# Gated loop attention with a multiplicative feed-forward: the looks wait for unit 0's last gated product, and unit 3's pieces begin after fifteen halves

## The chip, the cores and the metric

The kernel runs on one core of one Trainium2 chip. Its time is the device time of one execution in microseconds, and the median of several runs is compared. A profile of one more execution gives the start and length of every instruction on the engines: TensorE (PE, with its weight loads as PEld), VectorE (DVE), ScalarE (ACT), GpSimd (POOL) and SyncE (SP), which here only issues DMAs.

## What is computed

```python
def _attn_ref(q, k, v, a_re, a_im):          # (4, 8, 768, 48) each
    mag = np.sqrt(a_re * a_re + a_im * a_im)
    scale = np.minimum(mag, 0.999) / (mag + 1e-06)
    a_re_n, a_im_n = (a_re * scale, a_im * scale)
    for t in range(S):
        new_re = ar * S_re - ai * S_im
        new_im = ar * S_im + ai * S_re
        kv = np.einsum('bhd,bhe->bhde', k[:, :, t], v[:, :, t])
        S_re, S_im = (new_re + kv, new_im)
        y[:, :, t] = np.einsum('bhd,bhde->bhe', q[:, :, t], S_re)

def _moe_ref(x, w1, w2, w3, w_out):          # x: (3072, 384)
    a = x @ w1                               # 384 -> 1024
    b = x @ w2
    h = a * b @ w3                           # 1024 -> 1024
    return (h @ w_out).astype(np.float32)    # 1024 -> 384
```

A linear recurrence with a complex gate for each channel and step (the gate's magnitude is kept below 0.999) gives y. Its heads, put side by side, are the rows x of a feed-forward part in which two projections are multiplied element by element and then go through w3 and w_out.

## The kernel before

The 4 x 768 steps are cut into eight units of 384 steps, two for each batch entry, and each unit into three chunks of 128 steps. The weights come as 64-bit words and are rounded to 32 bits on the chip while the first 100 us run; w3 and w_out are multiplied into one matrix w3o.

Four kinds of work belong to each unit, and those of neighbouring units overlap:

- The gates (function gates): a chain of about thirty steps on ScalarE and VectorE over tiles of 128 x 1152. For unit u+1 it begins with two ScalarE passes over the real part (lines 594 and 596), then im times a factor (line 600, after the transfer of the imaginary part), its square (line 604), and a logarithm of that on ScalarE (line 609; a helper, line 586, records all these ScalarE steps). Later come scans (lines 628 and 687), products with k and q (654 and 656), and four products with cosine and sine (717, 719, 723 and 726). The transfer of the next unit's imaginary part is issued on SP's queue behind line 719, the moves of the finished tiles into the layout KL and QL behind that (line 736).
- The pieces: transposes of the scaled keys (line 766) with a ScalarE copy KT for each (768), the state products kv (830) with an addition on VectorE (836), the scores sc (780) with a masked copy (783), and the outputs y (813) with a ScalarE copy xT (815). Transposes, kv and y share two PSUM buffers (pool ps_v), so each of them waits until the copy of the last but one is out.
- The feed-forward: sixteen halves of three matmuls each (line 852). Halves of the first kind end in a ScalarE copy a (857), those of the second in the gated product ab on VectorE (859). Unit 0's output part is plain matmuls o (948). In the other units two tiles are done together with seven products p1, p2, p4, p6, p7, p5 and p3 in place of eight (912), for which VectorE forms four sums So (887).
- The looks (check_weights): GpSimd goes over all weights and the first two units' gates in 84 groups. It loads each with its own DMA queue (1042 and 1045), tests it in two to four operations (1066 to 1071) and adds up in the tile seen (1050); nothing else runs on GpSimd in that time. Near the end the function judge reads seen on VectorE (1170), sums over partitions on TensorE (1177) and sets a flag by which a general version is run if a test failed.

The order of TensorE's work is written out by hand. The function unit(u, rest, ahead) takes the pieces of unit u and the feed-forward items of unit u-1, puts the first `ahead` items in front, and spreads the pieces evenly among the others; the list AHEAD gives that number for each unit. A planner (run, with book, fits and fill) then goes through that sequence with a clock for each engine and the durations in TIMES, and puts the gate steps of the next unit on ScalarE and VectorE, and the DMAs on SP, where by its clocks they fit. Instructions on one engine run in the order so found. The looks are a generator called from the same loop, first when unit 2's part has begun; on GpSimd they stand in order behind each other, whatever the planner's clocks say.

The memset that opens the looks (line 1034) writes seen into memory that the weights' rounding used, and so waits for the last rounding on VectorE (line 1014). Waits beyond what the data ask for can be put in by hand:

```python
def behind(ins, key):
    if key in last:
        tc.add_manual_dep(ins.ins, last[key].ins.name, BEHIND, reason="room")
```

where the dictionary last holds instructions that were noted under a key.

Of the kernel before, what the change touches and what calls it, by code (L numbers as in the profile page):

```python
# [17 lines left out]
OP = mybir.AluOpType  # L18
# [358 lines left out]
def kernel(  # L377
# [36 lines left out]
    nc = tc.nc  # L414
# [8 lines left out]
    KF = FF // P  # L423
# [5 lines left out]
    TT = S // 2  # L429
    UC = TT // C  # L430
    NU = 2 * B
    AHEAD = [0, 3, 12, 12] + [8] * (NU - 4)
    LO, HI = 32, D - 32
    PASS, WIDE, SCAN, LAND, SLACK, LATE, RING, LOOK, NEAR, EARLY = 1.17, 1.4, 1.05, 1.8, 0.7, 1.2, 8, 4.0, 4, 2
    LOOKS = 3
# [59 lines left out]
    g_t, L_t, xT_t, ab_t, T_t, KT_t = {}, {}, {}, {}, {}, {}  # L495
# [34 lines left out]
    last = {}  # L530
# [4 lines that stand above are left out]
# [309 lines left out]
    def ffn_ab(u, j):  # L844
        got = []

        def half(w):
            if j == 0 and not got:
                ab_t[u] = one.tile([P, KF, TT], FP, tag="ab", name="ab")
            m = ps_m.tile([P, TT], FP, tag="mm", name="m")  # L850
            for f in range(KD):
                nc.tensor.matmul(out=m, lhsT=w[:, j * P // WB, f, j * P % WB:j * P % WB + P], rhs=xT_t[u][:, f],  # L852
                                 start=(f == 0), stop=(f == KD - 1))
            with tc.high_priority():
                if not got:
                    got.append(two.tile([P, TT], FP, tag="a", name="a"))
                    nc.scalar.copy(out=got[0], in_=m)  # L857
                else:
                    nc.vector.tensor_tensor(out=ab_t[u][:, j], in0=m, in1=got[0], op=OP.mult)  # L859
        return [("ab1", lambda: half(w1s)), ("ab2", lambda: half(w2s))]  # L860


# [157 lines left out]
    def words(src):  # L1020
        return (src if src.dtype == FP else src.bitcast(I32)).rearrange("(i p) m -> p i m", p=P)
# [3 lines left out]
    def check_weights(late):  # L1025

        groups = [("gate", u, f, x) for u in range(2) for f in range(KD) for x in range(2)]
        for w in (w1, w2, w3t, wo):
            if w.dtype != FP:
                src = words(w)  # L1030
                step = next(n for n in range(512, 0, -2) if src.shape[2] % n == 0)
                groups += [(w, src[:, i, j:j + step], step) for i in range(src.shape[1]) for j in range(0, src.shape[2], step)]
        seen = s_t["seen"] = late.tile([P, 256], BF, name="seen")
        nc.gpsimd.memset(seen, 0.0)  # L1034

        def load(group):
            got = late.tile([P, 512], FP, tag="look", name="look", bufs=LOOKS)
            if group[0] == "gate":
                _, u, f, x = group
                b, h = divmod(u, 2)  # L1040
                t0 = h * TT + x * (TT // 2)
                nc.gpsimd.dma_start(out=got[:, 0:TT // 2], in_=art[b, :, DG * f:DG * (f + 1), t0:t0 + TT // 2].rearrange(
                    "h d s -> d h s"))
            else:
                nc.gpsimd.dma_start(out=got.bitcast(I32)[:, 0:group[2]], in_=group[1])  # L1045
            return got

        def add(x):
            n = x.shape[1]
            nc.gpsimd.tensor_tensor(out=seen[:, 0:n], in0=seen[:, 0:n], in1=x, op=OP.add)  # L1050
            counted[0] += n

        tt, ts = nc.gpsimd.tensor_tensor, nc.gpsimd.tensor_scalar
        raws = [load(group) for group in groups[:LOOKS - 1]]
        for i, group in enumerate(groups):
            yield
            if i + LOOKS - 1 < len(groups):
                raws.append(load(groups[i + LOOKS - 1]))
            raw = raws.pop(0)
            if group[0] == "gate":  # L1060
                n = TT // 2
                x, y, low, high = raw[:, 0:n], raw[:, n:2 * n], SMALL, LARGE
            else:
                w, src, step = group
                x, y, low, high = raw[:, 1:step:2], raw[:, 0:step:2], MIN_SQ, MAX_SQ if w is w3t else None
                tt(out=x, in0=x, in1=x, op=OP.mult)  # L1066
            if high is not None:
                ts(out=y, in0=x, scalar1=high, scalar2=None, op0=OP.is_le)  # L1068
            ts(out=x, in0=x, scalar1=low, scalar2=None, op0=OP.is_ge)  # L1069
            if high is not None:  # L1070
                tt(out=x, in0=x, in1=y, op=OP.mult)  # L1071
            add(x)
# [14 lines left out]
    got = {}  # L1087
# [113 lines left out]
    def ffn(u, parts=1):  # L1201
        ab = [x for j in range(KF) for x in ffn_ab(u, j)]
        last = [(("o", "half")[parts - 1] if n == parts - 1 else "part", f) for n, f in enumerate(ffn_out(u, UC - 1, parts))]
        if u == 0:
            return ab + [(("part", "half")[n], f) for t in range(UC) for n, f in enumerate(ffn_out(u, t, parts))]


        def pair(*tiles):
            return [(f"p{p}", f) for p, f in zip((1, 2, 4, 6, 7, 5, 3), out_pair(tiles))]

        own, thirds = ((u, 0, False), (u, 1, False)), ((u - 1, UC - 1, True), (u, UC - 1, False))
        if u == 1:
            return ab + [("so", lambda: (out_sums(own), last[0][1]()))] + pair(*own)
        got = ab + [("sum", lambda: out_sums(own))] + pair(*own)
        if u % 2:
            return got + [("sum", lambda: out_sums(thirds))] + pair(*thirds)
        return got[:len(ab) + 6] + [("keep", lambda: keep(u))] + got[len(ab) + 6:]
# [8 lines left out]
    def unit(u, rest, ahead):  # L1226

        if u == 1:
            return [("begin", u)] + mixed([x for p in pieces(u) for x in p], rest, FILLS[1])
        seq = [("begin", u)] + rest[:ahead]  # L1230
        rest = rest[ahead:]
        p = pieces(u) + [[]]
        n = len(p)
        first = [i * (len(rest) - 2) // (n - 1) for i in range(n)] + [len(rest)]
        for i in range(n):
            seq += rest[first[i]:first[i + 1]] + p[i]
        return seq
# [175 lines left out]
    with tc.manual_schedule(engines={mybir.EngineType.PE}):  # L1413
# [30 lines left out]
        with tc.manual_schedule(engines={mybir.EngineType.Activation, mybir.EngineType.DVE, mybir.EngineType.Pool, mybir.EngineType.SP}):  # L1444

            paced.append(True)
            clock.update(PE=0.0, ACT=0.0, DVE=0.0, POOL=0.0, SP=3.0, DMA=8.0)
            landings[:] = [0.0] * RING
            ready.clear()
            ready.update({"moves": 9.0, ("raw", 0): 0.0, ("re", 1): 2.0})  # L1450
            w12_load(0, slice(len(got) and got[0][0][0].stop, KD))
            turn_v(0)
            w12_load(1)
            rest = ffn(0, 2)
            urgent.append([None, w12_ops()])

            def head(i):
                if i % 4 == 0:
                    force(i // 4)
                rest[i][1]()  # L1460
                if i == HEAD - 4:
                    phase.close()
                    late.append(fast.enter_context(tc.tile_pool(name="late", bufs=1)))
                    late.append(fast.enter_context(tc.tile_pool(name="looks", bufs=1)))
                    looks.append(check_weights(late[1]))
                    streams.append((1, out_weights()))
            seq = mixed([x for p in pieces(0) for x in p], fills, FILLS[0]) + [("begin", 0)] + [(rest[i][0], lambda i=i: head(i)) for i in range(HEAD)]
            for u in range(1, NU):
                seq += unit(u, rest[HEAD:] if u == 1 else ffn(u - 1), AHEAD[u])
            seq += ffn(NU - 1)  # L1470
            advance()
            run(seq[:-12] + [("judge", 0)] + seq[-12:-10] + [("judge", 1)] + seq[-10:])
# [41 lines left out]
```

## Time and profile before

| what | time, us |
|---|---|
| median of 3 runs | 552.43 (551.7 to 552.54) |
| the profiled execution | 552.92 |
| its span in the profile | 551.1 |
| TensorE busy | 521.0 |
| VectorE, ScalarE, GpSimd busy | 372.6, 275.3, 358.0 |
| looks: first instruction, last one's end | 105.2, 512.2 |

The span leaves out about 1.8 us of the execution. A share of busy time is a mean over the run, so the stages are read apart. Times are counted from the span's start:

| stage | us | TensorE busy | VectorE | ScalarE | GpSimd |
|---|---|---|---|---|---|
| start: weights, unit 0's gates | 0 to 72 | 54.95 | 58.55 | 58.29 | 2.36 |
| unit 0's pieces | 72 to 96 | 23.28 | 21.58 | 16.45 | 0.00 |
| feed-forward of unit 0, pieces of unit 1 | 96 to 146 | 46.88 | 31.50 | 26.85 | 33.45 |
| of unit 1, unit 2 | 146 to 205.1 | 59.07 | 43.14 | 30.00 | 50.45 |
| of unit 2, unit 3 | 205.1 to 262.1 | 54.63 | 40.95 | 32.87 | 50.12 |
| of unit 3, unit 4 | 262.1 to 325.4 | 63.01 | 51.87 | 33.43 | 56.79 |
| of unit 7, and the end | 495.5 to 551 | 49.50 | 16.32 | 4.46 | 14.18 |

The stages of units 5 to 7 that are left out are like that of unit 4: TensorE is busy in all but 0.4 us of each. Idle time of another engine costs nothing unless TensorE waits for it later.

### The profile page before, as it was taken

What the parts mean: (1) busy time and instruction counts of PE and PEld (TensorE: products, weight loads), DVE (VectorE), ACT (ScalarE), POOL (GpSimd) and SP (SyncE); (2) the same over time, 40 slices, a digit from 0 to 9 for tenths busy, and PEclk for the clock granted to TensorE, in tenths of its full rate; (3) what the DMA queues carried; (4) which work ended last, traced back from release to release, by engine and by line L of the source; (5) the groups of instructions that cost most, each with busy time, mean ns of one, the idle gap of its engine ahead of it and who ended that gap; (6) DMA issues with size and microseconds to landing.
All of it is one profiled execution on the core that took longest, in us unless ns stands there. A gap on an engine that the chain in (4) does not pass through costs nothing.

```text
span 551.1 us, 13443 instructions
## 1 busy us (share of the span) xinstructions
PE 521.0 (95%) x5546; PEld 370.0 (67%) x5546; DVE 372.6 (68%) x553; ACT 275.3 (50%) x391; POOL 358.0 (65%) x425
## 2 busy tenths in 40 slices
PE   4689899989999999989999999999999999999995
PEld 2345575556756795669568985687569966795585
DVE  5999589775585677867977985687669751531152
ACT  5989766465543555746467426743494232111100
POOL 1000000188888788888998888988998888888100
PEclk9899899999999999989999999999999999999999
DMA  8997956966659835492889346935793173222001
GB/s 262 339 395 236 212 167 189 253 161 162 159 141 242 223 106 132 146 207 84 245 212 218 112 129 165 215 110 152 170 224 100 58 205 83 73 65 96 1 26 39
DMA packets 73510, 89.73 MB, mean 163 GB/s; under 512 B 31840, under 2 KB 63264, under 8 KB 72672
## 3 DMA queue, kind: packets, MB, share of 16 engines
q1 hardware_dynamic: 67360, 69.78, 48.2%
q0 software_dynamic: 6080, 19.01, 11.7%
q8 instruction: 45, 0.74, 0.6%
q14 instruction: 25, 0.20, 0.1%
HBM read 65.14 MB, written 4.72 MB: 127 GB/s over the span
## 4 chain that ended last, share of the span: by engine, by line
PE 67%; DVE 14%; DMA 8%; ACT 5%; issue 3%; SPq 1%; DVEq 0%; ACTq 0%
PE m L852 35%; PE p L912 14%; PE y L813 6%; PE sc L780 5%; PE o L948 3%; DMA im<-in_a_im_dram 2%; DMA QL<-q 2%; DMA raw<-in_w_dram 2%; DVE gZ L687 2%; PE kv L830 2%; PE tp L766 2%; ACT low L1002 1%; DVE So L887 1%; DMA out_dram<-ot 1%; ACT gZ L586 1%
## 5 line engine op out<-in xcount | busy, mean ns | idle before, releaser
L852 PE MATMUL m<-xT,w1s 128*128 128x384 f32 x384 | 134.5, 487 | 1.1 <-ACT xT L815 1.1
L852 PE MATMUL m<-xT,w2s 128*128 128x384 f32 x384 | 134.8, 487 | 0.0
L852 PEld LDWEIGHTS m<-xT,w1s 128*128 128x128 f32 x384 | 72.2, 190 | 48.9 <-ACT xT L815 1.7
L852 PEld LDWEIGHTS m<-xT,w2s 128*128 128x128 f32 x384 | 71.9, 190 | 47.8
L1069 POOL TENSOR_SCALAR look<-look 128x256 f32<-128x256 f32 (+1 forms) x84 | 86.7, 1032 | 7.3
L1050 POOL TENSOR_TENSOR seen<-seen,look 128x256 bf16<-128x256 bf16 (+1 forms) x84 | 80.9, 963 | 6.8
L859 DVE TENSOR_TENSOR ab<-m,a 128x384 f32<-128x384 f32 x64 | 35.2, 551 | 69.8 <-PE m L852 66.3
L857 ACT COPY a<-m 128x384 f32<-128x384 f32 x64 | 30.2, 473 | 95.1 <-PE m L852 95.1
L1034 POOL MEMSET seen<- 128x256 bf16 x1 | 0.3, 311 | 102.3 <-DVE w2s L1014 102.3
L1068 POOL TENSOR_SCALAR look<-look 128x256 f32<-128x256 f32 (+1 forms) x44 | 51.7, 1174 | 6.1 <-DMA look<-in_a_re_dram 2.8
L1066 POOL TENSOR_TENSOR look<-look 128x256 f32<-128x256 f32 (+1 forms) x72 | 48.6, 675 | 3.5 <-DMA look<-in_w_dram 1.7
L912 PE MATMUL p<-To,So 128*128 128x192 f32 x240 | 44.1, 332 | 0.0
L1045 POOL DMA_DIRECT2D look<-in_w_dram x56 | 33.1, 591 | 16.6 <-POOL seen L1050 16.6
L815 ACT COPY xT<-y 128x384 f32<-128x384 f32 x24 | 11.5, 478 | 60.2 <-PE y L813 60.2
L1071 POOL TENSOR_TENSOR look<-look 128x256 f32<-128x256 f32 (+1 forms) x44 | 38.1, 866 | 3.7
L912 PEld LDWEIGHTS p<-To,So 128*128 128x128 f32 x240 | 38.7, 190 | 2.2 <-issue 2.0
L768 ACT COPY KT<-tp 128x384 f32<-128x384 f32 x40 | 34.0, 857 | 11.9 <-PE tp L766 11.7
L813 PE MATMUL y<-A,V 128*32 128x128 f32 x768 | 39.8, 273 | 0.1
L783 DVE COPY_PREDICATED A<-mask,sc 128x512 f32<-128x512 uint8 x48 | 32.7, 733 | 6.4 <-PE sc L780 6.2
L813 PE MATMUL y<-QL,T 96*32 96x128 f32 x640 | 35.5, 272 | 0.8 <-issue 0.8
L813 PEld LDWEIGHTS y<-A,V 128*32 128x32 f32 x768 | 34.3, 110 | 2.1 <-issue 2.0
L1150 PE MATMUL f<-wo_s,w3s 128*128 128x384 f32 x96 | 35.6, 520 | 0.0
(129 smaller groups left out, 922.4 us busy)
## 6 DMA issues: line engine op xcount, KB each, us to landing
look<-in_w_dram POOLq DMA_DIRECT2D x56, 256.0 KB, 4.0
raw<-in_w_dram SPq DMA_DIRECT2D x6, 1024.0 KB, 10.7
KL<-gR SPq DMA_DIRECT2D x24, 192.5 KB, 4.6
KL<-k SPq DMA_DIRECT2D x24, 192.5 KB, 6.1
re<-in_a_re_dram SPq DMA_DIRECT2D x24, 192.0 KB, 4.4
im<-in_a_im_dram SPq DMA_DIRECT2D x24, 192.0 KB, 4.0
k<-in_k_dram SPq DMA_DIRECT2D x24, 192.0 KB, 8.1
q<-in_q_dram SPq DMA_DIRECT2D x24, 192.0 KB, 7.4
```

The lines of the kernel that those rows point to most:

```text
L768: nc.scalar.copy(out=KT_t[u, c][:, :, :, x].rearrange("p h d f -> p f d h"), in_=tp.rearrange("p f (d h) -> p f d h", h=H))
L813: nc.tensor.matmul(out=o, lhsT=a, rhs=b, start=s0, stop=s1)
L852: nc.tensor.matmul(out=m, lhsT=w[:, j * P // WB, f, j * P % WB:j * P % WB + P], rhs=xT_t[u][:, f], start=(f == 0), stop=(f == KD - 1))
L859: nc.vector.tensor_tensor(out=ab_t[u][:, j], in0=m, in1=got[0], op=OP.mult)
L912: nc.tensor.matmul(out=m[p], lhsT=a[:, f], rhs=b[:, f], start=(f == 0), stop=(f == KH - 1))
L1045: nc.gpsimd.dma_start(out=got.bitcast(I32)[:, 0:group[2]], in_=group[1])
L1050: nc.gpsimd.tensor_tensor(out=seen[:, 0:n], in0=seen[:, 0:n], in1=x, op=OP.add)
L1066: tt(out=x, in0=x, in1=x, op=OP.mult)
L1068: ts(out=y, in0=x, scalar1=high, scalar2=None, op0=OP.is_le)
L1069: ts(out=x, in0=x, scalar1=low, scalar2=None, op0=OP.is_ge)
L1071: tt(out=x, in0=x, in1=y, op=OP.mult)
L1150: nc.tensor.matmul(out=sums[j], lhsT=w3_t[f][:, j * P:(j + 1) * P], rhs=w3_t["wo"][:, f], start=(f == 0), stop=(f == KF - 1))
```

## The change

Three edits. The gated product of each half is noted in last under the key ("ab", unit, number). The memset that opens the looks gets a wait by hand on unit 0's last gated product, the eighth; all looks and their loads stand behind it on GpSimd. And AHEAD for unit 3 becomes 15 where it was 12: fifteen items of unit 2's feed-forward stand ahead of the items among which unit 3's pieces are spread, so that the pieces share the ten items left in place of thirteen.

```diff
@@ -429,7 +429,7 @@
     TT = S // 2
     UC = TT // C
     NU = 2 * B
-    AHEAD = [0, 3, 12, 12] + [8] * (NU - 4)
+    AHEAD = [0, 3, 12, 15] + [8] * (NU - 4)
     LO, HI = 32, D - 32
@@ -856,7 +856,7 @@
                     got.append(two.tile([P, TT], FP, tag="a", name="a"))
                     nc.scalar.copy(out=got[0], in_=m)
                 else:
-                    nc.vector.tensor_tensor(out=ab_t[u][:, j], in0=m, in1=got[0], op=OP.mult)
+                    last["ab", u, j] = nc.vector.tensor_tensor(out=ab_t[u][:, j], in0=m, in1=got[0], op=OP.mult)
         return [("ab1", lambda: half(w1s)), ("ab2", lambda: half(w2s))]
@@ -1031,7 +1031,7 @@
         seen = s_t["seen"] = late.tile([P, 256], BF, name="seen")
-        nc.gpsimd.memset(seen, 0.0)
+        behind(nc.gpsimd.memset(seen, 0.0), ("ab", 0, KF - 1))
 
         def load(group):
```

The planned order of the built kernel shows what this does to each engine. GpSimd and SP issue the same instructions in the same order. On TensorE the sixteen halves of unit 2 come first and then unit 3's two first transposes, p1, the third transpose, kv, p2, the fourth transpose, p4, kv and p6. Before, the first transposes stood between the last three halves, and p6 stood behind the first scores. On ScalarE the last two copies a and the logarithm of unit 4's gates (line 609) come ahead of all four copies KT, where it stood between the second and the third; on VectorE the four sums So come ahead of the first addition to the state. Outside unit 3's part the orders are the same.

## The prediction

> **What bounds the kernel now.** I read the page first (busy shares), then the waits of TensorE by stage, then the timeline round the two longest of them, then the granted clock in one-microsecond steps, and last where GpSimd's looks begin and end. On the page TensorE (PE) is busy for 95% of the span, no other compute engine for more than 68%, and its clock is full in nearly every slice:
>
> ```profile
> PE 521.0 (95%) x5546; PEld 370.0 (67%) x5546; DVE 372.6 (68%) x553; ACT 275.3 (50%) x391; POOL 358.0 (65%) x425
> PEclk9899899999999999989999999999999999999999
> ```
>
> So behind the start-up (the first 72 us) a change pays only where it removes one of TensorE's few idle gaps, or time in which its clock is halved. The waits by stage give two gaps over 1 us: 1.47 us at 119 to 120.5, and 2.37 us at 237.9 to 240.3. First the looks and the first gap:
>
> ```profile
> 105.20 0.31 POOL L1034 MEMSET seen<- 128x256 bf16 x1 [102.26 <-DVE w2s L1014]
> 112.00 1.50 DVE L719 TENSOR_TENSOR gA<-q,re 128x1152 f32<-128x1152 f32 x1
> 113.42 1.75 DVE L723 TENSOR_TENSOR k<-k,gZ 128x1152 f32<-128x1152 f32 x1
> 118.50 1.50 DVE L600 TENSOR_TENSOR im<-im,gR 128x1152 f32<-128x1152 f32 x1 [1.25 <-DMA im<-in_a_im_dram]
> 119.92 0.55 DVE L859 TENSOR_TENSOR ab<-m,a 128x384 f32<-128x384 f32 x1
> 120.52 0.91 PE L948 MATMUL o<-w3o,ab 128*128 128x384 f32 x2 [1.47 <-DVE ab L859]
> ```
>
> The columns are start, length, engine, line, operation, and in brackets the idle time before it with what ended it. The memset that opens the looks starts at 105.20. The last gated product of unit 0 (L859 at 119.92) stands behind L600 on VectorE (DVE), which stands behind a transfer; TensorE waits for it. Now the second gap:
>
> ```profile
> 229.28 1.18 SPq L512 DMA_DIRECT2D im<-in_a_im_dram  x2
> 235.04 1.39 DVE L600 TENSOR_TENSOR im<-im,gR 128x1152 f32<-128x1152 f32 x1 [1.82 <-DMA im<-in_a_im_dram]
> 236.47 1.72 DVE L604 CUSTOM_DVE_ANT_0 gZ<-im 128x1152 f32<-128x1152 f32 x1
> 238.23 1.25 ACT L586 ACTIVATE gZ<-gZ,consts 128x1152 f32<-128x1152 f32 x1 [2.89 <-DVE st_tan L604]
> 239.39 0.82 ACT L768 COPY KT<-tp 128x384 f32<-128x384 f32 x1
> 240.27 0.55 PE L766 MATMUL tp<-ident,k 128*128 128x128 f32 x3 [2.37 <-ACT KT L768]
> ...
> 242.00:243.00 1.00, 1.00 (x23) 0.56 (x25) 0.24 (x1) 0.32 (x1) 0.97 (x2) 0.50 1.00 264
> ```
>
> The chain is: im transfer of unit 4, L600, L604, the Ln on ScalarE (ACT), the copy of unit 3's third transpose queued behind that Ln, and only then the buffer for the fourth transpose. The last line is from the table of stretches; its last three figures are the granted clock (0.50), the DMA share and GB/s. The clock is 0.78 in the stretch from 241 and 0.5 from 242 to 245, so for some 3.4 us after the gap matmuls ran at half speed. Its cost is read from the rows: p took 1.88 where 1.47 is usual, kv 1.50 where 0.88 is, the next p 2.09 where 1.47 is: 1.65 us. The second gap thus costs 2.37 + 1.65 = 4.0 us, the first 1.5. At the end:
>
> ```profile
> 511.64 0.54 POOL L1050 TENSOR_TENSOR seen<-seen,look 128x192 bf16<-128x192 bf16 x1
> 531.04 0.42 DVE L1170 SCALAR_TENSOR_TENSOR ok<-seen,consts 128x256 f32<-128x256 bf16 x1
> ```
>
> The looks end at 512.2, and what reads them (L1170) runs at 531.04: 18.9 us of room.
>
> **What the Trainium skill says.** SBUF — State Buffer, section Who interferes with whom: a VectorE instruction with two inputs in SBUF and a GpSimd instruction that reads SBUF exclude each other, and whoever starts second is blocked. The trace agrees: L723 takes 1.36 us in one unit and up to 1.84 in others, and GpSimd's 192-wide test 0.69 to 1.75. TensorE: Matmul & The Clock Gate, section What's actually happening: after at least one idle window of about 3.4 us the clock is halved. Here 2.1 us of idle in one such stretch was enough, and the 1.47 us gap at 120 was not (clock 1.00 behind it). DMA: Bandwidth & Descriptors, section Issuing engines are not separate DMA queues: transfers of SP and POOL share 16 engines. The trace agrees: from 234 to 245 their busy share is 1.0 or above, with looks and moves in it. Perfetto Trace Analysis, section GPSIMD Engine Instruction: take GpSimd's times from start to start; I do so below.
>
> **Part 1, the looks begin later.** The added wait stands on the memset. Behind it on GpSimd are the looks alone, 84 groups, and their DMAs (POOL's own queue); nothing but the judgement at the end waits for them. SP's queue is not passed by anything. The wait can't fall out for lack of its key: the looks are first called in unit 2's part of the order, when unit 0's products are on record. The memset now starts when L859 at 119.92 has ended: near 120.3 instead of 105.2, 15 us later.
>
> What it takes away: the blocking of VectorE between 112 and 120. L719 took 1.50 and L723 1.75; undisturbed each is 1.36 (L717, just ahead, and the least of other units). The im transfer starts after L719, so it gains 0.14; L600 goes from 1.50 to 1.39 or 1.36, 0.14. The gated product then ends 0.3 us earlier, and TensorE's gap shrinks by 0.3. Bounds: 0.1 (the transfer lands no earlier) and 0.6 (one look transfer of 96 KB less on the queue). I take 0.3. VectorE's other gains (L723 0.4, L726 0.35) hide under the transfer, for VectorE idles 1.25 us before L600.
>
> What it moves: every look from here on meets other VectorE work. Start to start, the looks from memset to end last 407 us. With each kind at its undisturbed spacing they would last 325, so 82 us is blocking, at about 4 us in each 15 us up to 450 and almost none after. The first 15 us hold 4.0 of it, which are exchanged for 15 us at the end with about none: 407 - 4 = 403, from 120.4 to 523. That is 8 us before 531, so the later start is hidden.
>
> The second gap moves too, since it is at the end of a chain of VectorE steps (213.97 on) in which unit 3 was blocked more than the others. The three scans L687 took 3.98 against 3 x 1.08 in the other odd units (0.74 more), L690 0.47 against 0.30 (0.17), L656 1.76 against a mean of 1.58 (0.18), L719 1.83 against 1.49 (0.34), L702 1.57 against 1.60 (-0.03): 1.40 ahead of the im transfer. Then L600 1.39 against 1.49 (-0.10) and L604 1.72 against 1.45 (0.27). With the looks 15 us away I take the means: L604 ends not at 238.20 but 1.57 earlier, and 0.3 earlier still from the first gap, since its chain starts at a TensorE result: 236.3. Bounds: 238.3 (as blocked as before or slightly more) and 235.0 (blocked nowhere).
>
> **Part 2, twelve halves to fifteen.** In the planned order the three halves that stood between unit 3's first transposes now come ahead of them. The orders of SP and GpSimd stay as they are, only some tile buffers are numbered otherwise. TensorE runs 16 halves (204.98 + 16 x 1.936 = 235.95), two transposes (0.33 each), p1 (1.40), and stands at the third transpose at 238.0, or 237.7 with part 1. On ScalarE the last a copy and the Ln now come ahead of all four KT copies. So the third transpose waits for the first KT copy, which ends 2.0 us behind L604's end (Ln 1.16 to its successor, copy 0.85), and kv waits for the second copy, 0.85 later, of which the transpose covers 0.33. The wait is there in both orders, at the same distance behind L604. The new order has done p1 (1.40) ahead of it where the old one had done kv (0.82), which gives 0.58, and loses 0.83 for the second copy: 0.25 worse, if L604 stays where it is. By itself the part is no gain.
>
> Behind it: the fourth VectorE sum So is now ahead of the states T, and p6 ahead of the scores. With L604's end at E, kv ends at E + 3.9, So at E + 3.7, T at E + 4.5, scores start at E + 9.1 = 245.4. The last QL piece landed near 245.8 to 246.5 and follows the im transfer, 1.7 us earlier: 244.1 to 244.8, just in time. I put 0.3 us on that closeness.
>
> **The sum.** With E = 236.3 TensorE waits 0.7 us (238.4 against 237.7) and then 0.5. That is 1.2 in all, less than the gap at 120 that left the clock alone; so no half clock. Stage: 4.0 - 1.2 = 2.8; first gap 0.3; less 0.3: 2.8 us. From 262 on TensorE idles under 1 us up to the end (waits by stage), so the gain reaches the end. The profiled run took 552.92 (span 551.1); 550.1 by the sum, and from the median 552.43: 549.6.
>
> **Rivals.**
> Blocking just as bad (0.22). Looks still run through 205 to 242, and 4 us per 15 is the level everywhere. If E comes only to 237.5 or 238, the waits are 2.0 to 2.9 and the half clock stays: 0.3 to 0.7 gained, 0.25 lost, about 552.2. For it: L723 took over 1.7 in five of seven units. Against it: the scans were 0.74 above the others in this unit alone.
>
> The moved pieces make it slower (0.12). Both KT copies stand behind the Ln, so TensorE idles twice with 0.33 us of work between. If E stays at 238.0 or later, that is 2.4 + 0.5 us instead of 2.4, and these can spoil two clock windows in place of one: 0.25 + 1.7 us, 554.4. It decides from about E = 238. For it: ScalarE's order puts Ln ahead of all copies. Against: E must lose nothing of 1.9 us.
>
> The looks become the last thing (0.03). If they end after 528 (531 less the gain), VectorE stands at L1170, the sums and the count matmul behind it, and each microsecond costs one: 5 us more blocking than worked out, then 553 to 555. Against it: 8 us of room.
>
> **How the numbers follow.** The main case has 0.63, with 548.2 to 551.2 as its own range (E from 235 to 237). The three runs shown lie within 0.15% of each other; 0.2% is 1.1 us, about what a measurement can tell from no change. Faster: 0.63 and a little of the first rival, 0.65; the same: 0.20; slower: 0.12 + 0.03. The range reaches over the first rival, 548.1 to 552.8.
>
> **What would show it.** The memset at 120 with its wait on L859; L719 and L723 near 1.36 between 112 and 115; the gap at 120 near 1.2; L604 of the fourth unit's gates ending before 237; two waits of TensorE for KT copies behind p1, together under 1.5 us, and a clock of 1.00 through 240 to 246; the looks' end near 523. I am wrong if L604 still ends at 238, if the clock falls in that stage, or if a new gap over 1 us opens in a later unit.

## The result, and the profile after

| | median, us | executions | ratio to before, 95% interval |
|---|---|---|---|
| before | 552.59 (549.64 to 556.68) | 16 | |
| changed | 548.71 (545.06 to 554.02) | 16 | 0.9936 (0.9913 to 0.996) |

The changed kernel is faster by 3.5 us, 2.2 to 4.8 by the interval. The forecast was 2.8 us. Some executions of every kernel are slower as a whole, and the ratios leave these out, so they differ a little from the quotient of the medians. The profiled execution took 550.05 (span 548.1), that of before 552.92 (span 551.1).

Two single profiles can't be subtracted as wholes here. Of the 3.0 us between these spans, 2.2 are there before the change has acted: line 717, the first product with sine or cosine in unit 1's gates, starts at 108.49 where it started at 110.72. Before that the order is the same in both; 0.85 us was gained ahead of unit 0's feed-forward, most of the rest is one transfer of raw weights that came 1.28 us late in the profile of before. Over the fourteen profiles of this study (of the kernels before and changed, of their repeats and of the variants below) the first half of unit 0's feed-forward begins anywhere from 77.0 to 86.9 us. So below each stage is measured from its own first half of feed-forward.

The page of the changed kernel, busy shares and granted clock:

```profile
PE 518.6 (95%) x5546; PEld 368.5 (67%) x5546; DVE 374.4 (68%) x553; ACT 275.2 (50%) x391; POOL 358.3 (65%) x425
PEclk9899899999999999999999999999999999999999
```

The 8 in the eighteenth slice, which was the half clock behind the second gap, is gone; TensorE is 2.4 us less busy for the same 5546 matmuls. The timeline of the changed kernel round the first gap (start, length, engine, line, operation, and in brackets the idle time before it and what ended it):

```profile
109.77 1.35 DVE L719 TENSOR_TENSOR gA<-q,re 128x1152 f32<-128x1152 f32 x1
111.04 1.35 DVE L723 TENSOR_TENSOR k<-k,gZ 128x1152 f32<-128x1152 f32 x1
116.48 1.36 DVE L600 TENSOR_TENSOR im<-im,gR 128x1152 f32<-128x1152 f32 x1 [2.35 <-DMA im<-in_a_im_dram]
117.76 0.55 DVE L859 TENSOR_TENSOR ab<-m,a 128x384 f32<-128x384 f32 x1
118.36 0.31 POOL L1034 MEMSET seen<- 128x256 bf16 x1 [115.42 <-DVE ab L859]
118.36 0.91 PE L948 MATMUL o<-w3o,ab 128*128 128x384 f32 x2 [0.16 <-DVE ab L859]
```

The memset starts when the eighth gated product is out, so the wait does what it says. The three gate products are down to 1.35 and 1.36 from 1.50, 1.75 and 1.50. TensorE's wait is 0.16 where it was 1.47; with this one pair that is mostly the late start of the other profile; a mean over several profiles follows below. The second gap in the changed kernel:

```profile
232.47 1.36 DVE L600 TENSOR_TENSOR im<-im,gR 128x1152 f32<-128x1152 f32 x1 [1.56 <-DMA im<-in_a_im_dram]
233.86 1.47 DVE L604 CUSTOM_DVE_ANT_0 gZ<-im 128x1152 f32<-128x1152 f32 x1
235.37 1.25 ACT L586 ACTIVATE gZ<-gZ,consts 128x1152 f32<-128x1152 f32 x1 [2.92 <-DVE st_tan L604]
236.53 1.52 ACT L768 COPY KT<-tp 128x384 f32<-128x384 f32 x2
237.40 0.55 PE L766 MATMUL tp<-ident,gR 128*128 128x128 f32 x3 [1.58 <-ACT KT L768]
242.85 1.57 PE L912 MATMUL p<-To,So 128*128 128x192 f32 x8
245.11 1.57 PE L780 MATMUL sc<-QL,KL 96*32 96x128 f32 x64 [0.70 <-issue]
```

Both KT copies now stand behind the logarithm (235.37), as worked out from the order. TensorE waits 1.58 us for the first and then, with p6 (242.85) already done, 0.70 at the scores. The word "issue" stands where the profile names nothing that ended a wait; the last move into QL landed at 244.8, just ahead of these scores. Unit 3's stage, 56.97 us from the first half of unit 2's feed-forward to the first of unit 3's, is 55.90. The end of the looks:

```profile
524.44 1.00 POOL L1050 TENSOR_TENSOR seen<-seen,look 128x192 bf16<-128x192 bf16 x1
528.42 0.42 DVE L1170 SCALAR_TENSOR_TENSOR ok<-seen,consts 128x256 f32<-128x256 bf16 x1
```

They end at 525.4, 3.0 us before they are read; 18.9 were left before.

### The profile page after: what moved, and what is told of

Its sections match the earlier page's. It is cut to its first block, busy times and chain, and to the rows that moved or that the text cites. A ratio compares the mean times of both kernels' runs of the same rounds, so it can differ in the third digit from the quotient of the medians.

```text
span 548.1 us, 13443 instructions
## 1 busy us (share of the span) xinstructions
PE 518.6 (95%) x5546; PEld 368.5 (67%) x5546; DVE 374.4 (68%) x553; ACT 275.2 (50%) x391; POOL 358.3 (65%) x425
## 4 chain that ended last, share of the span: by engine, by line
PE 78%; DVE 9%; ACT 5%; issue 3%; DMA 3%; SPq 1%; DVEq 0%; ACTq 0%
PE m L852 37%; PE p L912 16%; PE y L813 7%; PE sc L780 5%; PE f L1150 3%; PE o L948 3%; PE kv L830 3%; PE tp L766 2%; DMA im<-in_a_im_dram 1%; DVE gZ L687 1%; PE sc L1150 1%; ACT gZ L586 1%; DMA raw<-in_w_dram 1%; ACT re L586 1%; ACT low L1002 1%
## 5 line engine op out<-in xcount | busy, mean ns | idle before, releaser
L1069 POOL TENSOR_SCALAR look<-look 128x256 f32<-128x256 f32 (+1 forms) x84 | 90.2, 1074 | 7.3
L1050 POOL TENSOR_TENSOR seen<-seen,look 128x256 bf16<-128x256 bf16 (+1 forms) x84 | 75.8, 902 | 6.8
L1068 POOL TENSOR_SCALAR look<-look 128x256 f32<-128x256 f32 (+1 forms) x44 | 51.0, 1160 | 7.5 <-DMA look<-in_a_re_dram 4.3
L1066 POOL TENSOR_TENSOR look<-look 128x256 f32<-128x256 f32 (+1 forms) x72 | 52.8, 733 | 1.9
L1045 POOL DMA_DIRECT2D look<-in_w_dram x56 | 33.2, 592 | 16.6 <-POOL seen L1050 16.6
L1071 POOL TENSOR_TENSOR look<-look 128x256 f32<-128x256 f32 (+1 forms) x44 | 36.2, 824 | 3.7
```

## The experiments

Three theories were put against each other. W: the later looks bring the gain by themselves. A: the fifteen halves do. B: each needs the other. All edits below are against the kernel before or after, as named; ratios are to the kernel before, run on the same chip.

**One part at a time.** The wait alone:

```diff
-    AHEAD = [0, 3, 12, 15] + [8] * (NU - 4)
+    AHEAD = [0, 3, 12, 12] + [8] * (NU - 4)
```

> The wait alone, AHEAD for unit 3 at 12. Theory W (the later looks bring the gain): 2.5 to 3.5 us below before, unit 3's stage without half clock. Theory A (the fifteen halves bring it): within 0.5 us of before, the wait of the fourth transpose for the KT copy near 2.4 us with a half-clock window behind it. Theory B (both are needed): 0.3 to 1 us below before.

The fifteen halves alone: the kernel before with 15 in that list.

> Fifteen halves alone, looks as before. Theory W and the prediction's step on part 2: 0 to 0.5 us above before, the wait at the third transpose over 2 us. Theory A: 2 to 3.5 us below before, no half clock in unit 3's stage. Theory B: 0.3 to 1 us below.

Measured: the wait alone 552.25, ratio 0.9994 (0.997 to 1.0018); the fifteen halves alone 550.78, 0.998 (0.9958 to 1.0002). Neither shows a gain that its interval separates from none. Theory W, which asked for 2.5 to 3.5 us from the wait alone, is excluded by its interval; theory A is not, since the interval of the fifteen halves alone reaches to 2.3 us. The timeline of the wait alone:

```profile
239.63 0.55 PE L766 MATMUL tp<-ident,k 128*128 128x128 f32 x3 [1.26 <-ACT KT L768]
247.12 1.67 PE L780 MATMUL sc<-QL,KL 96*32 96x128 f32 x64 [2.04 <-DMA QL<-q]
248.72 2.84 PE L912 MATMUL p<-To,So 128*128 128x192 f32 x8
```

The wait for KT has come down to 1.26, but TensorE reaches the scores before QL has landed, stands 2.04 us, and the clock falls: p takes 2.84 where 1.57 is usual. The stage lasts 58.03. The timeline of the fifteen halves alone:

```profile
241.28 0.55 PE L766 MATMUL tp<-ident,gR 128*128 128x128 f32 x3 [3.00 <-ACT KT L768]
242.78 2.86 PE L912 MATMUL p<-w3o,ab 128*128 128x192 f32 x8
```

Here the scores don't wait, since p6 stands ahead of them, but the wait for KT is 3.00 with the half clock behind it: 57.85. In these two profiles each part of the change shortens one wait of unit 3's stage and leaves or lengthens the other. Two more things happen in the profile of the fifteen halves alone. The transfer of unit 4's imaginary part lands 5.4 us behind its last issue where it took 4.2 in the repeat of the kernel before, so the logarithm is late for a reason that isn't the order of the halves. And the first gap, 1.98 us there, is followed by half clock too.

**Without looks.** To see what the looks cost at most, by blocking and by their transfers, all groups of looks are left out, so that neither weights nor gates are tested; once with twelve and once with fifteen halves:

```diff
+        groups = []
         seen = s_t["seen"] = late.tile([P, 256], BF, name="seen")
```

> All looks are left out (GpSimd does nothing between 72 us and the end), AHEAD 12. It measures what all blocking of VectorE and all DMA traffic by looks cost. By the prediction's step on blocking, L604 of unit 4's gates then ends 2 to 3 us earlier against TensorE's halves, the wait at the fourth transpose falls under 0.5 us, no half clock, and the time is 4 to 5 us below before. If blocking isn't what makes the wait, the wait stays at 2 us or more and the time is within 1 us of before.

> The same without looks, AHEAD 15. If the order of the halves costs 0.25 us only while ScalarE's Ln is late, this equals the run with 12 within 0.3 us; theory A: 1 to 3 us below the run with 12.

Measured: 544.37, ratio 0.9863 (0.9835 to 0.989), and 544.76, 0.9879 (0.9848 to 0.991). The looks cost about 7 us in all, where 4 to 5 were expected, and without them no difference between twelve and fifteen halves can be seen (seven and six executions). The timeline with fifteen:

```profile
211.16 2.83 DVE L687 TENSOR_TENSOR_SCAN gZ<-im,st_ang 128x384 f32<-128x384 f32 x3 [0.42 <-ACT im L586]
224.79 1.35 DVE L723 TENSOR_TENSOR k<-k,gZ 128x1152 f32<-128x1152 f32 x1
231.40 1.36 DVE L604 CUSTOM_DVE_ANT_0 gZ<-im 128x1152 f32<-128x1152 f32 x1
235.08 0.49 PE L766 MATMUL tp<-ident,gR 128*128 128x128 f32 x3
241.82 1.32 PE L780 MATMUL sc<-QL,KL 96*32 96x128 f32 x64
```

No bracket stands at the transposes or the scores: TensorE waits for nothing, and the stage lasts 52.76. L604 ends 30.6 us behind the stage's first half; in the profile of before 33.2. So of the 7 us that the looks cost, about 5 lie in this one stage (52.8 and 53.2 without them, a mean of 57.8 before); unit 4's (62.97 against 63.35 to 63.68) and unit 6's (62.80 against 63.40 to 64.01) hold 0.4 to 1.2 each.

Blocking and transfers are both gone here, and the traces separate them in part. Without looks the last issue of unit 4's imaginary part, which stands behind line 719, comes 24.0 us behind the stage's first half in place of 25.5. So 1.5 of the 2.6 us by which L604 ends earlier lie in work on VectorE ahead of the transfer. The last move into QL is issued 31.8 us behind the first half in place of 33.8, and lands in 6.2 us in place of 8.0. For the scores the looks' transfers thus cost about as much as the blocking, by this pair of profiles. No run leaves out the one and keeps the other.

**The same kernels again.** The changed kernel twice and the kernel before once more, unchanged, for how far one profile can be trusted.

> The changed kernel once more, for a second profile of it and a time beside the variants. If the wait and the fifteen halves only pay together: 2 to 4 us below before, unit 3's stage near 56 us with a wait for a KT copy near 1.6 us, a short wait ahead of the scores, and the clock full. If the first figure was scatter: 0.5 to 1.5 us below before.

> The kernel before against itself, for a second profile of it and for what the timing can tell apart: ratio 1.000 with an interval of 0.25% to each side; unit 3's stage 56.5 to 58 us with a KT wait over 2 us and a half-clock window in it.

> The changed kernel a third time. If it gains 2 to 3 us by both parts together: ratio 0.994 to 0.997, unit 3's stage 55.9 to 56.6 us, a KT wait near 1.6 us. If the first figure was scatter: ratio 0.998 or above.

Measured: the changed kernel 549.35, ratio 0.9967 (0.9941 to 0.9994), and 550.1, 0.9985 (0.9958 to 1.0013); the kernel before 551.24, 1.0009 (0.9982 to 1.0035). Weighted by their precision, the three comparisons of the changed kernel give 0.9960 with half an interval of 0.0015, which is 2.2 us, give or take 0.8. But the three scatter more than their own intervals let one expect (3.5, 1.8 and 0.8 us), so that by their scatter the half interval is nearer 1.6 us; the two repeats alone give 1.3, give or take 1.1. The first 3.5 us was on the high side.

All profiles by stage, from first half to first half of the feed-forward; the waits are TensorE's in unit 3's stage:

| kernel | unit 3's stage | unit 4's | waits in unit 3's stage | half clock there |
|---|---|---|---|---|
| before | 56.97 | 63.35 | KT 2.4 | 3.4 us |
| before again | 58.61 | 63.68 | KT 2.4, scores 1.5 | 3.4 |
| changed | 55.90 | 64.24 | KT 1.6 and 0.2, scores 0.7 | no |
| changed again | 56.55 | 63.45 | KT 1.6 and 0.2 | 3.4 |
| changed, third | 56.89 | 64.27 | KT 2.2 and 0.2, scores 0.5 | no |
| wait alone | 58.03 | 63.74 | KT 1.3, scores 2.0 | yes |
| fifteen alone | 57.85 | 63.53 | KT 3.0 and 0.2 | yes |
| no looks, twelve | 53.19 | 62.86 | KT 0.1 | no |
| no looks, fifteen | 52.76 | 62.97 | none | no |
| p6 ahead, twelve | 56.35 | 64.69 | KT 1.2, scores 1.7 | no |
| paused, twelve | 54.34 | 66.36 | KT 0.4, scores 0.6 | no |
| paused, fifteen | 54.06 | 64.16 | KT 0.2 | no |
| paused, fifteen again | 53.18 | 64.25 | KT 0.2 | no |
| looks still later | 59.34 | 63.87 | KT 4.2 | 6.8 |

Unit 3's stage has a mean of 57.8 before and 56.45 after, but the single values nearly touch (56.97 and 56.89). A stretch of half clock, 3.4 us at half speed, costs TensorE 1.7 us. It stands in both profiles of before and in one of three of the changed kernel, which makes 1.1 of the 1.35 us between the means; less this, the stages are 55.3 and 56.9 before, 55.9, 54.9 and 56.9 after. The five profiles thus don't show that the two waits together have become shorter. Nor can they tell how often the half clock comes: over 177 executions of the kernel before and 41 of the changed kernel the mean granted clock is 0.9868 and 0.9878, which makes 0.5 us of an execution, give or take 0.7.

**p6 ahead without the fifteen halves.** If fifteen halves help only because p6 comes ahead of the scores and covers the landing of QL, the wait with twelve halves and p6 moved by hand must do the same (the planner then moves some gate steps on VectorE as well):

```diff
+        if u == 3:
+            kinds = [kind for kind, _ in seq]
+            seq.insert(kinds.index("sc"), seq.pop(kinds.index("p6")))
```

> The looks' wait of the change with AHEAD 12, and the product p6 put by hand ahead of unit 3's first scores (as fifteen halves put it). If the part of the fifteen halves is that p6 covers the wait of the scores for QL: that wait falls from 2.0 us to under 1, and the time is 1.5 to 3 us below before, as for the whole change. If it is the place of the halves against the transposes: as with the wait alone, within 1 us of before.

Measured: 550.27, ratio 0.9998 (0.9973 to 1.0023). The timeline:

```profile
233.06 0.55 PE L766 MATMUL tp<-ident,k 128*128 128x128 f32 x3 [1.18 <-ACT KT L768]
238.35 1.46 PE L912 MATMUL p<-To,So 128*128 128x192 f32 x8
241.49 1.32 PE L780 MATMUL sc<-QL,KL 96*32 96x128 f32 x64 [1.67 <-issue]
```

The stage is as short as the changed kernel's (56.35), but the scores still wait 1.67, and the median shows no gain. All the waits of the stage come to 3.2 us where the wait alone had 3.3; the stage is 1.7 us shorter because the clock happened to stay full. So this run doesn't show p6 to be the cover that makes the fifteen halves pay, and what they do beside the wait stays open.

**Looks that pause while unit 3's gates run.** No wait at the start; instead the 24th group of looks waits for the last of unit 3's four products with cosine and sine:

```diff
-            tt(out=q, in0=q, in1=Z, op=OP.mult)
+            last["qs", u] = tt(out=q, in0=q, in1=Z, op=OP.mult)
...
+            while i == 24 and ("qs", 3) not in last:
+                yield
...
-                tt(out=x, in0=x, in1=x, op=OP.mult)
+                first = tt(out=x, in0=x, in1=x, op=OP.mult)
+                if i == 24:
+                    behind(first, ("qs", 3))
```

With twelve halves:

> The looks begin as before and stop once, ahead of group 24, until line 726 of unit 3's gates has run (about 17 us in which these gates' steps and the moves run undisturbed); AHEAD 12. If blocking and shared DMA engines in just this stretch make the late transfer, Ln and moves: L604 ends 31 us or less behind the stage's first half (33.2 before), unit 3's stage 53.5 to 54.5 us in place of 57, time 2.5 to 4 us below before. If the looks cost by their number anywhere: within 1 us of before. The looks would end near 524, 3 us ahead of their reading; if they are late, the tail loses what they overrun.

With fifteen, and once more in another set of runs:

> The same pause with AHEAD 15. If the fifteen halves matter only as cover of late KT copies and late moves, this equals the pause with 12 within 0.5 us; if they gain by themselves, 1 us or more below it.

> The pause with AHEAD 15 again, beside the changed kernel. If the stretch of unit 3's gates is where the looks hurt most: 1 to 3 us below the changed kernel, unit 3's stage near 54 us. If not: level with the changed kernel.

Measured: twelve 548.61, ratio 0.9981 (0.9954 to 1.0008); fifteen 546.81, 0.9928 (0.9895 to 0.9962), and 547.75, 0.995 (0.9922 to 0.9978). The timeline with fifteen (its lines 1068 and on are 1066 and on of the kernel before):

```profile
211.47 3.25 DVE L687 TENSOR_TENSOR_SCAN gZ<-im,st_ang 128x384 f32<-128x384 f32 x3 [0.43 <-ACT im L586]
223.83 1.35 DVE L719 TENSOR_TENSOR gA<-q,re 128x1152 f32<-128x1152 f32 x1
225.10 1.35 DVE L723 TENSOR_TENSOR k<-k,gZ 128x1152 f32<-128x1152 f32 x1
228.28 0.60 POOL L1068 TENSOR_TENSOR look<-look 128x256 f32<-128x256 f32 x1 [15.30 <-DVE q L726]
236.29 0.88 PE L830 MATMUL kv<-vr,KT 128*32 128x48 f32 x48 [0.15 <-ACT KT L768]
242.53 1.76 PE L780 MATMUL sc<-QL,KL 96*32 96x128 f32 x64
```

GpSimd stands still for 15.30 us, as long as the wait of the change delays it, but in another place. The products run at 1.35, L604 ends 31.0 behind the stage's start, and TensorE's waits are down to 0.15. The stage falls to 54.06 and 53.18, near that without looks. With twelve halves it falls as well (54.34), but unit 4's stage takes 66.36, with waits of 1.1, 0.7 and 0.6 us, and most of it is given back, so that the median is 1 us below before where 2.5 to 4 were expected; why was not tried. The two runs with fifteen make 0.9941 with half an interval of 0.0021, 3.2 us faster than before. That is the best version run. Beside the changed kernel in the same two sets of runs it is 2.2 us faster, give or take 1.0 (by the means of the executions), and its stage is 2 to 4 us shorter. The pause takes the looks' transfers out of this stretch as well as their blocking. The pause and the wait together were not run.

**Looks later still.** The memset waits for a masked copy of unit 1's scores, 13 us later yet:

```diff
-        behind(nc.gpsimd.memset(seen, 0.0), ("ab", 0, KF - 1))
+        behind(nc.gpsimd.memset(seen, 0.0), ("sc", 1, 0, 1))
```

> The changed kernel with the looks' wait moved from unit 0's last gated product to the second masked copy of unit 1's first chunk, some 14 us later. By the prediction's third rival the looks then end near 538, some 10 us behind the point (528) at which VectorE comes to read them, and the time rises by 7 to 11 us over the changed kernel, with TensorE waiting at the count matmul. If the end has more room than worked out: within 1 us of the changed kernel.

Measured: 554.57, ratio 1.0054 (1.0025 to 1.0083): slower. The timeline:

```profile
131.42 0.76 POOL L1034 MEMSET seen<- 128x256 bf16 x1 [128.48 <-DVE A L783]
239.51 0.90 PE L766 MATMUL tp<-ident,gR 128*128 128x128 f32 x3 [4.16 <-ACT KT L768]
532.86 0.55 POOL L1050 TENSOR_TENSOR seen<-seen,look 128x192 bf16<-128x192 bf16 x1
533.44 0.42 DVE L1170 SCALAR_TENSOR_TENSOR ok<-seen,consts 128x256 f32<-128x256 bf16 x1 [1.36 <-POOL seen L1050]
```

Now the looks are read the moment they end, and TensorE's count behind that waits 1.6 us for VectorE. Against the changed kernel more of the loss is in unit 3's stage: 59.34, with a wait for KT of 4.16 and two stretches of half clock. There the transfer of unit 4's imaginary part took 6.7 us to land where it took 4.0 to 4.2 in the changed kernel, so this wait is one for a transfer. The kernel is 4.5 us slower than the changed one's third median where 7 to 11 were expected: the looks end at 533.4, not near 538.

## Why the prediction was right, and where its steps were not

The side was right, and the size fits: 2.8 us were forecast, the three comparisons give 2.2. But the way there was right only at the first gap. The largest term, an L604 that ends 1.57 us earlier because unit 3 is blocked less, did not come true, so that the sum came near is in good part luck: the waits stayed, and in two of three profiles the half clock did not come. Of the three signs by which the prediction called itself wrong, one stayed away in the first profile, for L604 ended at 235.3 and not at 238 (most of that was the earlier start of the whole profile). The other two came: the clock fell in unit 3's stage in one of three profiles, and a new wait over 1 us opened in a later unit in all three. By its steps:

1. **The first gap: 0.3 forecast, about 0.6 measured.** From the start of line 717 to the end of the eighth gated product it takes 9.75, 10.11, 10.34, 10.45, 9.99 and 10.07 in the six profiles with early looks, 9.82, 9.21, 9.59, 9.37, 9.65 and 9.26 in the six with the later memset: means 10.12 and 9.48, so 0.64, give or take 0.3. The mechanism was right: the gate products are at 1.35 in all six. The term was mis-sized because one profile stood for all: L719, taken at 1.50, has a mean of 1.65 in the six, so that it gains 0.30 and not 0.14; L717, taken as undisturbed, has a mean of 1.52 and gains 0.16; the transfer behind them is 0.13 shorter, L600 gains 0.05. TensorE's wait there has a mean of 1.5 in the first six (0.3 to 2.0) and 0.5 in the others (0 to 1.5). It depends on when TensorE arrives too, so that mean is rough.

2. **The moved pieces: not contradicted.** By themselves 0.25 worse and no gain was forecast; fifteen halves alone has the stage at 57.85 against a mean of 57.8 before. Its wait for KT of 3.0 has the late transfer in it, and its median allows a gain, so this one profile doesn't settle the term. The QL moves "just in time", 0.3 us: 0.7, 0 and 0.5 in the three profiles. That p6 ahead of the scores is what keeps this wait short is not shown: without it the scores stood 2.04 with the wait alone and not at all in the first profile of before, and with it they stood 1.67 in the run with twelve halves.

3. **Unit 3's blocking falls to the mean of the other units: wrong.** This is the step that failed. L604 was to end 1.57 us earlier for it. From the stage's start it ends at 33.22 and 33.23 in the kernel before, 32.60, 32.65 and 33.23 in the changed one: 0 to 0.6 earlier, from L600, L604 and the landing of the transfer ahead of them. The scans are as blocked as ever. The timelines of the two kernels, first the changed one:

```profile
207.81 1.77 POOL L1066 TENSOR_TENSOR look<-look 128x256 f32<-128x256 f32 x1
209.68 1.93 POOL L1069 TENSOR_SCALAR look<-look 128x256 f32<-128x256 f32 x1
211.74 4.01 DVE L687 TENSOR_TENSOR_SCAN gZ<-im,st_ang 128x384 f32<-128x384 f32 x3 [0.43 <-ACT im L586]
217.90 1.76 DVE L656 TENSOR_TENSOR q<-q,gA 128x1152 f32<-128x1152 f32 x1
225.19 1.83 DVE L719 TENSOR_TENSOR gA<-q,re 128x1152 f32<-128x1152 f32 x1
```

and the kernel before:

```profile
210.05 1.77 POOL L1066 TENSOR_TENSOR look<-look 128x256 f32<-128x256 f32 x1
211.91 1.91 POOL L1069 TENSOR_SCALAR look<-look 128x256 f32<-128x256 f32 x1
213.97 3.98 DVE L687 TENSOR_TENSOR_SCAN gZ<-im,st_ang 128x384 f32<-128x384 f32 x3 [0.43 <-ACT im L586]
```

The stages begin at 202.74 and 204.98, so both first lines stand at 5.07, with the same length, although three or four groups fewer have been done by then; L687 (4.01 and 3.98), L656 (1.76) and L719 (1.83) repeat too. In all five profiles of the two kernels it is so. The three profiles with a pause have this relation too, up to the pause. The other four with looks show just two more: the wait alone and p6 ahead share one (first test at 4.28 and 4.31, L687 3.38 and 3.39), and fifteen alone and looks still later share another (3.43 and 3.44, L687 3.85), though the looks of these two begin some 30 us apart. So twelve profiles fall into three relations, and neither the delay nor the count of groups done selects one; what does was not found. Within the changed kernel the memset stands 84.0 to 84.5 us ahead of the stage's start, and the tests still coincide to 0.02 us: what differs at the start is gone by then. The Trainium skill, SBUF — State Buffer, section Who interferes with whom, has a blocked instruction wait until the other is through. If that happens in both directions, as the lengths of both engines here suggest, each collision sets the two engines to the same relation again, and a delay doesn't draw a new one. That the places repeat, and that the stream comes back to them, is shown; that this is the way is argued.

4. **The waits of 0.7 and 0.5 without a half clock: half right.** They came to 1.7 to 2.4 for KT. The rule used for the clock, that less idle than the first gap's 1.47 leaves it alone, could not be tried at 1.2, and the length of a gap alone doesn't decide (last section). In the sum, 2.8 for the stage became 1.35 (57.8 to 56.45), most of it a half clock that came in two of two profiles before and in one of three after. Unit 4's stage gives 0.5 back, a mean of 63.99 where it was 63.52; in two of the changed kernel's three profiles its scores wait 1.0 and 1.2 us for a masked copy on VectorE, a wait of 0.3 and 0.4 before. In the third the same kind of wait, 1.3 us, stands in unit 6's stage.

5. **The looks' length: 403 forecast, 407.1, 404.6 and 407.6 measured,** so 3.0 us of room in the first profile in place of 8. The saving of 4 us fits: the kernel before has 407.0 and 413.9, the fifteen halves alone 410.3, and the mean falls from 410.4 to 406.4. The start of 407 was a low one, again because one profile stood for all.

So of the pooled 2.2 us, 0.6 are found in the chain to the first gap and 0.9 between unit 1's and unit 7's feed-forward (unit 3's stage less what unit 4 and others give back; means 350.07 and 349.20). Unit 0's whole stage is 1.1 shorter in the mean (63.0 twice before; 61.6, 63.2 and 61.1 after), so that the first gap may hold some of the other 0.7, but its values scatter by 2 us. That the two parts need each other (theory B) is not shown. The stages of the two parts alone (58.03 and 57.85) are longer than the changed kernel's chiefly because both have a stretch of half clock; less this they are 56.3 and 56.1, inside the changed kernel's 54.9 to 56.9. The intervals of the fifteen halves alone and of the changed kernel overlap, so the times don't settle it either.

The rivals: "blocking just as bad" was true of the blocking, and still a gain came: the first gap was worth 0.6, and the half clock, which this rival kept, stayed away in two of three profiles. "The moved pieces make it slower" needed L604 as late as before; fifteen halves alone has it later still and is not slower. "The looks become the last thing" was 3 us away, not 8, and looks still later show it, with VectorE waiting 1.4 us for them and a worse unit 3 besides.

## What to carry to other kernels

Ask of background work not how much room it has in all but which stretch it collides with: with fifteen halves, the same 15 us of stillness on GpSimd was worth 1.3 us in unit 3's stage when it came at the start, a figure within the scatter of the profiles, and about 4 when it came while that unit's gates ran. Don't expect a shifted stream to meet average conditions: price the stretch with it and without it. And where a chain and a transfer end close together, gaining on one of them alone can hand the wait to the other, as with the wait alone here.

Before a shorter stage is credited to an edit, count the stretches of half clock in it: one of them, 1.7 us, is more than the 1.35 us between the two kernels' means for unit 3's stage.

## What the runs showed of the hardware that was not expected

The repeat of two engines' places above: equal to 0.03 us after a delay of 15 us, and three relations in twelve profiles.

The clock doesn't go by the length of a gap. The Trainium skill, TensorE: Matmul & The Clock Gate, section What's actually happening, has the clock halved after at least one idle window of about 3.4 us. The changed kernel's second profile had the clock halved behind a shorter gap:

```profile
237.97 0.55 PE L766 MATMUL tp<-ident,gR 128*128 128x128 f32 x3 [1.64 <-ACT KT L768]
239.47 2.54 PE L912 MATMUL p<-w3o,ab 128*128 128x192 f32 x8
```

while its third profile had a longer gap and full clock:

```profile
237.81 0.55 PE L766 MATMUL tp<-ident,gR 128*128 128x128 f32 x3 [2.23 <-ACT KT L768]
239.33 1.57 PE L912 MATMUL p<-w3o,ab 128*128 128x192 f32 x8
```

So a gap of 1.64 us halved the clock for about 3.4 us (p at 2.54 where 1.57 is usual), and one of 2.23 didn't. Neither is an idle window of 3.4 us.

The clock records of the traces say a good part of why. In each of the fourteen profiles every change of the granted clock lies on a grid with a step of 3.413 us, to within 0.002 us. What counts is how much of TensorE's idle time falls into one step of it:

| profile, wait | gap, us | most idle time in one step, us | clock in the next |
|---|---|---|---|
| p6 ahead, twelve: scores | 1.67 | 1.39 | 1.0 |
| changed, third: KT | 2.23 | 1.47 | 1.0 |
| before: first gap | 1.47 | 1.47 | 1.0 |
| before again: scores | 1.49 | 1.49 | 0.5 |
| before again: KT | 2.39 | 1.58 | 1.0 |
| changed again: KT | 1.64 | 1.63 | 0.5 |
| paused, twelve: first gap | 2.04 | 1.87 | 1.0 |
| fifteen alone: first gap | 1.98 | 1.98 | 0.5 |
| wait alone: scores | 2.04 | 2.04 | 0.5 |
| before: KT | 2.37 | 2.12 | 0.5 |

From 100 to 500 us, over all profiles, no step with up to 1.47 us of idle time was followed by half clock, and all five with 1.94 us or more were; in between both occur, and what decides there stays open. A gap that lies across an edge of the grid is split between two steps, as the 2.23 us of the third profile were. Where the edges fall changes from execution to execution. In planning, a gap of 2 us of a busy TensorE is to be priced with about half a chance of another 1.7 us: by these limits it is 0.45 to 0.7, an estimate from the figures above for a gap that falls anywhere on the grid.
